# Attention and gated convolution on one core: q and k loaded nine tokens a row, five score matmuls a head, and a new written order

## The chip, the cores and the metric

The kernel runs on one core of one Trainium2 chip. The metric is the device time of one launch in microseconds. A core has five engines that run side by side, each through its own list of instructions in order: PE (matrix multiply; its weight loads are listed as PEld), ACT (activation functions and copies), DVE (elementwise work), POOL (GpSimd, which has no access to PSUM here) and SP (which only issues DMAs). They wait for one another through semaphores. Data moves between device memory and the on-chip memory (SBUF) by 16 DMA engines. PE writes into PSUM, which has eight banks of 128 partitions x 512 fp32.

## The reference

Attention with a block-causal mask over 8 batches, 8 heads, 576 tokens and a head size of 64, and behind it a gated unit: a causal convolution over 5 tokens makes a gate, a projection makes the values, and their product is projected out.

```python
# attention: q, k, v are (8, 8, 576, 64)
scores = (1 / sqrt(64)) * q @ k.T                 # per batch and head
mask   = (pos_q // 64) >= (pos_k // 64)
attn   = softmax(where(mask, scores, -1e9))
x      = (attn @ v) put as (B, S, 512)            # heads side by side
# gated unit
gate = sigmoid(sum over k of conv_w[k] * x shifted by 4 - k tokens)   # zeros ahead of each batch
out  = (gate * (x @ w_val)) @ w_out               # (8, 576, 512) fp32
```

## The kernel before, in words

The unit of attention is a pair of heads: pair p = 4 b + g holds heads 2 g and 2 g + 1 of batch b, so there are 32 pairs. The two heads of a pair lie on partitions 0 to 63 and 64 to 127, and PE works on both side by side. All work is cut into steps, and PLAN, a text of some 990 words, gives their order by hand. A word is `step/arguments/engine/banks`: `S/4.1/P/4+5` is step S for pair 4, pass 1, on PE, into banks 4 and 5. The loop at the end of the kernel emits the steps in that order; each engine gets its own steps in the order of the list, and a step waits for the data that it reads and for the banks or buffers that it overwrites. The engines are P (PE), A (ACT), V (DVE), G (POOL) and S (SP).

The steps of a pair:

- `lq`, `lk`, `lv` (SP): load q, k, v into rings of staging tiles (`qks`, `vs`, five each). Only tokens 0 to 511 go this way, four tokens a row of 1 KB. `cq`, `cv` cast to fp16.
- `T`: 16 transposes (64 x 64) of q and k; `Te` copies the result from PSUM to `qkT`. The first pair that is read in halves uses `T0`, `T0e`, `cq0`.
- The tail path: tokens 512 to 575 of q and k of a whole batch are loaded by `lt`, cast by `ct`, turned by `TT`, copied by `TTe` into `ktails`.
- `S`: scores in three passes of 512 columns, with keys on the partitions. Pass 0 is one matmul a head (512 columns), pass 1 two (384 and 128), pass 2 five (256, and four of 64 columns for the tail queries). `E` takes the exponential of one pass (128 x 1024 elements) on ACT. `SL` and `EL` do the tail keys with the tail queries for the whole batch.
- `mka`, `mkb` (POOL): memsets that put the mask's zeros into the result of E.
- `A`: 20 matmuls of 65 columns, attention times v with a column of ones; `N` divides by that column. `AT`, `NT` do it for the tail queries of a batch.
- `X` (and `XT`): transposes of the result; `Xe`, `XTe` copy it into `xt`, a ring of four batches with four columns of zeros ahead of each.

The gated unit runs over `xt` in ten runs n of 464 columns: `C` (80 matmuls in 32 x 32 tiles, four banks) is the convolution, `CS` the tanh on ACT (two a run), `V` (four a run) the projection by w_val, `Ve` the product on DVE into `gv`. `O` projects 128 tokens by w_out, `Oe` copies to an output tile, `Od` stores it. `OL` is the last output in two halves. C of a run needs Xe of all pairs of the batches that it covers, and V, Ve and O follow it.

At the start `CW` (on PE) turns conv_w, which `lcv` loads and `ccv` casts. `lwo`, `cwo` load w_out and cast it; step `W` puts its rows into the order of use by 16 matmuls, and `We` brings it back from PSUM with a factor 0.5.

PSUM is mostly given out in pairs of banks. A helper, `place`, lets several small results share a pair: T and SL take half of it, X and TT a quarter, A three quarters.

All matmuls and transposes are recorded at the lines of two helpers (`mm`, L137; `turn`, L141), and all copies at L246 (DVE and POOL) and L244 (ACT), so the profile tells them apart by the names of what they read and write: S reads `qkT`, A reads `v,pt`, C reads `xt,DG`, V `xt,w_val`, O `w_out,gv`; Te writes `qkT`, Xe `xt`, Oe `osb`.

Of the kernel before, what the change touches and what calls it, by code (L numbers as in the profile page):

```python
# [12 lines left out]
lk/1/S ppool//G pdve//V lcv//S ccv//G CW//P/1 lq/1/A cq/1/V T/1/P/4+5 lq/0/S lk/0/S lt/0.1/S  # L13
lt/0.0/S ct/0/G lk/4/S lq/3/S CWe//V lk/3/S cq/3/G cq0/0/V T0/0/P/0+1 lq/2/S lk/2/S lq/4/S cq0/1/V
T0/1/P/2+3 Te/1/A pact//A S/1.1/P/4+5 lv/1.0/S lv/0.0/S lv/0.1/S S/1.0/P/6+7 lt/1.0/S lq/5/S
lv/2.1/S T0e/0/V lk/5/S T0e/1/A S/0.0/P/2+3 lv/1.1/S lv/2.0/S lvt/0/S lv/3.1/S lt/1.1/S TT/0/P/0+1
lk/6/S TTe/0/V lv/3.0/S lq/6/S cq/4/G E/1.1/A E/0.0/A lwv/1/S lwv/0/S SL/0/P/0+1 EL/0/A S/0.2/P/2+3
E/1.0/A S/1.2/P/4+5 E/1.2/A S/0.1/P/0+1 T/3/P/6+7 cq/2/V T/2/P/4+5 mka/1/G cv/0/G Te/3/A S/3.1/P/6+7
E/0.1/A T/4/P/0+1 Te/2/V S/2.2/P/4+5 lwo/1/S lwo/0/S E/0.2/A mka/0/G mkb/0/G lk/7/S S/2.1/P/2+3
lq/7/S lt/2.0/S Te/4/V S/4.0/P/0+1 E/3.1/A E/2.2/A E/2.1/A S/2.0/P/6+7 E/2.0/A A/0/P/4+5 S/3.2/P/6+7  # L20
cq/5/V T/5/P/2+3 lt/2.1/S lk/8/S lv/4.1/S lq/10/S E/4.0/A N/0/V cv/2/V X/0/P/4+5 mkb/1/G cv/1/G
A/1/P/0+1 lq/8/S Xe/0/V E/3.2/A S/4.1/P/4+5 N/1/V S/3.0/P/6+7 mkb/3/G mkb/2/G mka/2/G Te/5/A
S/5.0/P/2+3 lk/10/S E/4.1/A ct/1/G cv/3/G lv/4.0/S A/2/P/0+1 N/2/V lq/9/S lk/9/S lv/6.0/S E/3.0/A
mka/3/G S/5.1/P/4+5 E/5.1/A TT/1/P/6+7 TTe/1/V lv/5.1/S cvt/0/G cq/6/G A/3/P/0+1 N/3/V cwv/1/G
cwo/0/G E/5.0/A ct/2/G lv/7.1/S S/4.2/P/6+7 SL/1/P/4+5 lv/6.1/S EL/1/A mka/4/G cq/7/G E/4.2/A
mkb/4/G cq/8/G lq/13/S lv/5.0/S lv/7.0/S lvt/1/S lk/12/S lq/12/S lk/11/S lq/11/S AT/0/P/2 X/1/P/4+5
X/3/P/0+1 Xe/3/A T/6/P/6+7 Te/6/A X/2/P/0+1 Xe/2/A NT/0/V XT/0/P/3 S/6.0/P/6+7 E/6.0/A Xe/1/V
C/0/P/0+1+4+5 CS/0.1/A CS/0.0/A XTe/0/V cwv/0/V V/0.3/P/7 cwo/1/V Ve/0.3/V V/0.0/P/6 Ve/0.0/V
S/6.1/P/4+5 E/6.1/A W//P/0+1+2+3 We/0/A We/1/V S/5.2/P/6+7 TT/2/P/4+5 TTe/2/V V/0.2/P/2 SL/2/P/0+1
S/6.2/P/4+5 E/5.2/A T/7/P/6+7 Ve/0.2/V Te/7/V EL/2/A E/6.2/A V/0.1/P/0 S/7.0/P/4+5 E/7.0/A mka/5/G  # L30
T/8/P/6+7 S/7.1/P/2+3 E/7.1/A Ve/0.1/V cv/4/G A/4/P/0+1 Te/8/V S/8.2/P/6+7 N/4/V E/8.2/A O/0.2/P/4
Oe/0.2/A mkb/5/G S/8.1/P/0+1 E/8.1/A X/4/P/2+3 mka/6/G cq/10/G Xe/4/V cq/9/G T/9/P/6+7 T/10/P/6+7
Te/9/V S/8.0/P/4+5 E/8.0/A O/0.0/P/2 Oe/0.0/V S/7.2/P/0+1 E/7.2/A S/9.2/P/4+5 E/9.2/A cv/6/G mkb/8/G
Te/10/V mkb/6/G A/6/P/2+3 cv/5/G A/5/P/0+1 N/6/V mka/7/G S/9.0/P/6+7 S/9.1/P/4+5 E/9.0/A mkb/7/G
cv/7/G A/7/P/2+3 lk/13/S E/9.1/A lt/3.0/S N/5/V X/5/P/2+3 S/10.1/P/6+7 E/10.1/A lq/14/S lt/3.1/S
cvt/1/G AT/1/P/0 S/10.0/P/4+5 E/10.0/A O/0.1/P/1 Oe/0.1/A lk/14/S N/7/V Xe/5/V NT/1/V XT/1/P/0
X/6/P/6+7 Xe/6/A XTe/1/V X/7/P/2+3 cq/12/G T/12/P/4+5 cq/11/G T/11/P/4+5 lv/9.1/S S/10.2/P/0+1
E/10.2/A cq/13/G mka/9/G Xe/7/V C/1/P/2+3+6+7 lv/8.1/S CS/1.0/A ct/3/G cq/14/G mka/8/G Te/11/V
Te/12/V lv/8.0/S lq/15/S cv/8/G mkb/9/G V/1.0/P/1 Ve/1.0/V V/1.1/P/0 Ve/1.1/V CS/1.1/A lk/15/S
lv/9.0/S lt/4.1/S S/11.1/P/2+3 lvt/2/S lv/11.1/S lt/4.0/S E/11.1/A lv/11.0/S lk/17/S T/13/P/4+5  # L40
TT/3/P/4+5 lq/17/S lv/10.0/S lv/10.1/S lq/18/S lk/18/S Te/13/V S/11.0/P/6+7 E/11.0/A V/1.3/P/1
Ve/1.3/V T/14/P/2+3 Te/14/V mkb/10/G cv/9/G lv/12.0/S mka/11/G S/11.2/P/6+7 V/1.2/P/0 TTe/3/A
E/11.2/A S/13.1/P/4+5 mkb/11/G lv/12.1/S Ve/1.2/V S/14.1/P/2+3 S/13.2/P/6+7 cq/15/G A/8/P/0+1
E/13.1/A O/0.4/P/4 ct/4/G E/13.2/A S/13.0/P/6+7 N/8/V E/14.1/A lq/16/S lk/16/S Oe/0.4/V A/9/P/0+1
S/12.0/P/2+3 X/8/P/4+5 E/13.0/A T/15/P/4+5 N/9/V S/12.1/P/6+7 S/12.2/P/0+1 E/12.0/A E/12.1/A
lv/13.1/S Te/15/V Xe/8/V X/9/P/2+3 E/12.2/A cv/11/G A/11/P/2+3 N/11/V O/0.5/P/7 lt/6.1/S Oe/0.5/A
Xe/9/V S/14.0/P/5+6 mka/10/G cvt/2/G lv/13.0/S cq/17/G TT/4/P/0+1 T/17/P/0+1 X/11/P/0+1 Te/17/V
mka/12/G E/14.0/A S/14.2/P/2+3 cv/10/G cq/18/G AT/2/P/7 E/14.2/A O/0.3/P/6 Oe/0.3/A TTe/4/V Xe/11/V
# [64 lines left out]
def kernel(  # L113
# [57 lines left out]
    def both16(banks):  # L171
        return pick(PS16, banks)
# [569 lines left out]
```

## Time and profile before

| | |
|---|---|
| device time, 3 runs | median 184.38 us (183.89 to 184.41) |
| span of the profiled execution | 180.0 us |
| the profiled execution's own time | not recorded apart from the runs; its span and what lies around it make up the runs' 184.4 us |
| DMA | 40.39 MB in 66494 packets |
| chain that ended last | PE 59%, DMA 14%, SP's queue 9%, ACT 6% |

The span runs from the first to the last instruction; a run's time also holds what lies around it, here about 4.4 us. The profile gives each engine's busy time, its idle time with what ended it, and the chain of work that ended last, which is followed back from the last instruction. The chain holds PE almost without a break from 74 us on; before that it passes through DMA landings, SP's issues, ACT and DVE.

### The profile page before, as it was taken

The page shows a single profiled execution, that of the slowest core. Times are in us where ns is not written, and L with a number is a line of the kernel's source. Part 1 is how long each engine was busy: PE and PEld are TensorE (multiplying, and loading weights), DVE is VectorE, ACT ScalarE, POOL GpSimd, SP SyncE. Part 2 cuts the span into 40 slices and gives each one's busy share as a digit, 9 for nine tenths or more (in the row PEclk, how much of TensorE's full clock was granted, in tenths as well). Part 3 has the DMA queues.
Part 4 walks back from the last instruction along what each step waited for, and adds up shares of the span by engine and source line. Part 5 has one row for each costly group of instructions (what it writes and reads, how often), then busy time and mean ns, then how long its engine had stood idle before and what let it go on. Part 6 is the DMA issues. An engine that isn't in the chain of part 4 may idle for free.

```text
span 180.0 us, 8228 instructions
## 1 busy us (share of the span) xinstructions
PE 159.7 (89%) x3513; PEld 98.5 (55%) x3513; DVE 122.6 (68%) x249; ACT 137.3 (76%) x162; POOL 82.6 (46%) x198
## 2 busy tenths in 40 slices
PE   0567987779989998899899999999999999999991
PEld 0343765345754665656555755566775557455450
DVE  6635665687869786669748896587984876935640
ACT  2499999889979997989798989988996753333432
POOL 6326372677674677547467437462930622000000
PEclk9999999999999999999999999999999999999999
DMA  5899899997978799969999997998796006063366
GB/s 171 255 302 228 195 326 358 267 271 171 292 223 233 175 281 243 236 200 269 296 214 273 329 275 193 293 284 224 229 319 167 0 4 230 6 232 127 117 235 232
DMA packets 66494, 40.39 MB, mean 224 GB/s; under 512 B 40213, under 2 KB 60949, under 8 KB 66458
## 3 DMA queue, kind: packets, MB, share of 16 engines
q1 hardware_dynamic: 65898, 39.35, 76.0%
q8 instruction: 27, 0.44, 1.1%
q10 hardware_dynamic: 560, 0.52, 0.9%
q14 instruction: 9, 0.07, 0.1%
HBM read 30.42 MB, written 9.44 MB: 221 GB/s over the span
## 4 chain that ended last, share of the span: by engine, by line
PE 59%; DMA 14%; SPq 9%; ACT 6%; issue 4%; DVE 3%; POOL 2%; POOLq 0%; DVEq 0%
PE PS L137 54%; PE PS L141 5%; DMA qks<-in_q_dram 5%; ACT pt L458 4%; SPq L258 4%; DMA qks<-in_k_dram 3%; DMA vs<-in_v_dram 3%; SPq L281 3%; SPq L274 2%; DMA conv_nat<-in_moe_conv_w_dram 2%; DMA vts<-in_v_dram 2%; ACT qkT L244 1%; DVE x L509 1%; DVE qkT L246 1%; POOL qk L246 1%
## 5 line engine op out<-in xcount | busy, mean ns | idle before, releaser
L458 ACT ACTIVATE pt<-PS 128x1024 f16<-128x1024 f32 x96 | 93.1, 1041 | 10.6 <-PE PS L137 9.0
L246 POOL CAST qk<-qks 128x1024 f16<-128x1024 f32 x28 | 29.0, 1041 | 18.8 <-DMA qks<-in_k_dram 9.1
L137 PE MATMUL PS<-xt,w_val 128*128 128x464 f16 x160 | 36.5, 360 | 0.5 <-DVE w_out L600 0.3
L137 PE MATMUL PS<-qkT 64*128 64x256 f16 (+3 forms) x256 | 34.0, 319 | 3.0 <-DVE qkT L246 1.2
L137 PE MATMUL PS<-w_out,gv 128*128 128x512 f16 (+1 forms) x148 | 35.6, 374 | 0.0
L635 DVE SCALAR_TENSOR_TENSOR gv<-th,PS 128x112 f16<-128x112 f32 (+4 forms) x64 | 26.1, 449 | 10.2 <-ACT th L617 5.1
L137 PEld LDWEIGHTS <-pt 128*128 128x128 f16 (+1 forms) x960 | 28.0, 103 | 8.0 <-issue 4.0
L137 PE MATMUL PS<-v,pt 128*128 128x65 f16 (+1 forms) x896 | 31.4, 196 | 0.8 <-POOL v L246 0.3
L246 DVE COPY qkT<-PS 128x1024 f16<-128x1024 f16 (+1 forms) x24 | 28.7, 1199 | 4.7 <-PE PS L141 3.0
L137 PEld LDWEIGHTS <-qkT 64*128 64x128 f16 x512 | 17.5, 98 | 16.6 <-issue 9.4
L617 ACT ACTIVATE th<-PS 128x928 f32<-128x928 f32 x20 | 17.8, 947 | 9.9 <-PE PS L137 9.5
L246 POOL CAST v<-vs 128x512 f16<-128x512 f32 x31 | 19.2, 622 | 12.0 <-DMA vs<-in_v_dram 8.7
L509 DVE TENSOR_TENSOR x<-PS,rc 128x512 f16<-128x512 f32 x32 | 22.1, 692 | 1.1
L137 PEld LDWEIGHTS <-w_val 128*128 128x128 f16 x160 | 13.9, 98 | 14.1 <-issue 2.6
L137 PEld LDWEIGHTS <-gv 128*128 128x128 f16 x148 | 13.0, 98 | 13.3 <-issue 1.5
L246 DVE COPY osb<-PS 128x512 f32<-128x512 f32 x18 | 12.4, 690 | 7.6 <-PE PS L137 5.2
L141 PE MATMUL PS<-ident,qk 64*128 64x64 f16 x512 | 13.8, 199 | 3.9 <-POOL qk L246 1.3
L246 DVE COPY xt<-PS 128x512 f16<-128x512 f16 (+1 forms) x34 | 13.1, 399 | 5.4 <-PE PS L141 3.2
L481 POOL MEMSET pt<- 64x256 f16 x32 | 9.8, 306 | 14.0 <-ACT pt L458 13.0
L244 ACT COPY osb<-PS 128x512 f32<-128x512 f32 x17 | 10.0, 586 | 7.0 <-PE PS L137 4.5
L141 PEld LDWEIGHTS <-qk 64*128 64x128 f16 x512 | 11.1, 100 | 7.2 <-POOL qk L246 2.8
L508 DVE RECIPROCAL rc<-PS 128x8 f32<-128x8 f32 x32 | 6.6, 205 | 12.2 <-PE PS L137 9.6
(62 smaller groups left out, 134.3 us busy)
## 6 DMA issues: line engine op xcount, KB each, us to landing
out_dram<-osb SPq DMA_DIRECT2D x35, 256.0 KB, 3.3
qks<-in_k_dram SPq DMA_DIRECT2D x32, 256.0 KB, 4.7
vs<-in_v_dram SPq DMA_DIRECT2D x64, 128.0 KB, 4.3
qks<-in_q_dram SPq DMA_DIRECT2D x31, 256.0 KB, 4.6
tls<-in_k_dram SPq DMA_DIRECT2D x16, 64.0 KB, 4.1
tls<-in_q_dram SPq DMA_DIRECT2D x16, 64.0 KB, 3.6
vts<-in_v_dram SPq DMA_DIRECT2D x8, 128.0 KB, 4.0
gv<-in_moe_w_val_dram SPq DMA_DIRECT2D x2, 512.0 KB, 6.9
```

Source lines behind the costliest of these rows:

```text
L137: made.append(nc.tensor.matmul(out=out, lhsT=lhsT, rhs=rhs, start=start, stop=stop, skip_group_check=True))
L141: made.append(nc.tensor.transpose(out=out, in_=in_, identity=identity))
L244: i = nc.scalar.copy(out=out, in_=in_)
L246: i = (nc.vector if eng == "V" else nc.gpsimd).tensor_copy(out=out, in_=in_)
L258: DMA[eng].dma_start(out=rot(qks, p)[0:128, i], in_=(q, k)[i][b, 2 * g:2 * g + 2, 0:512, 0:64].rearrange("h (p n) d -> p h (n d)", n=4))
L281: DMA[eng].dma_start(out=tls[b % 2][0:128, i, r], in_=(q, k)[i][b, 0:8, 512:576, 0:64].rearrange("(g r) (p n) d -> r p g (n d)", r=2, n=2)[r])
L458: made.append(nc.scalar.activation(out=rot(pts, p)[0:128, 0:2, 512 * t:512 * t + 512], in_=both(take("S", p, t)), func=AF.Exp, bias=0.0, s ...
L481: nc.gpsimd.memset(pt[64:128, 0:2, 0:1024].rearrange("p h (t s) -> p h t s", t=2)[:, :, :, 0:64], 0.0)
L508: made.append(nc.vector.reciprocal(out=rc[0:128], in_=r[:, :, :, 64:65]))
L509: made.append(nc.vector.tensor_tensor(out=rot(x16, p)[0:128].rearrange("p i h d -> p h i d"), in0=r[:, :, :, 0:64], in1=rc[0:128].to_broad ...
L617: made.append(nc.scalar.activation(out=rot(ths, n)[0:128, 2 * i:2 * i + 2], in_=both(take("C", n, i))[:, :, 0:RUN], func=AF.Tanh, bias=0.0 ...
L635: made.append(nc.vector.scalar_tensor_tensor(out=gv[0:128, x, a - 4 * i:e - 4 * i], in0=rot(ths, n)[0:128, x, a - o:e - o], scalar=1.0, in ...
```

## The change

- q and k are loaded with nine tokens in a row of 2304 bytes, all 576 tokens at once. `lt`, `ct`, `TT`, `TTe`, `ktails` are gone. For batch 0, `lq` and `lk` load a pair with q on partitions 0 to 63 and k on 64 to 127. From batch 1 on, `lQ` loads four heads (two pairs) of q or of k into one staging tile by two DMAs; the pairs' rows lie on the two halves of the partitions.
- `c` (or `ch` by halves) casts a staging tile, T does 18 transposes of it, Te copies 128 x 1152 elements. From batch 1 on one T is q or k of two pairs, so scores of a pair need two T.
- S has the passes 512; 448 and 64; 192 and 320 columns: five matmuls a head. Each mask step is one memset.
- `lwo` loads w_out in the order of use (four DMAs), `cwo` casts it with the factor 0.5. `W` and `We` are gone.
- `place` is gone: T, X, A and SL take a pair of banks each.
- The written order is new for all engines. It has filler matmuls at the start (`w0`: 6, 3, 2 and 1 of 512 columns on 128 rows), `ccv` on ACT, more casts on DVE (six `c`, ten `cv` and four `cvt`; before three `cq` and one `cv`), and nine stores (`Od`) on ACT's queue.

The order up to the first S passes of batch 1, and around C/2 and C/3, in the new list:

```diff
+lcv//S ccv//A lk/0/S pact//A pdve//V w0/6.128.0/P/7 CW//P/0 ppool//G lq/0/S ch/0.0/G ch/0.1/V lk/1/S
+lq/1/S c/1/G CWe//V w0/3.128.0/P/7 T/0/P/2+3 Th/0.0/A Th/0.1/V w0/2.128.0/P/7 S/0.1/P/2+3 E/0.1/A
+S/0.2/P/0+1 T/1/P/4+5 E/0.2/A w0/1.128.0/P/7 S/0.0/P/2+3 E/0.0/A Te/1/V lk/2/S lq/2/S lq/3/S lk/3/S
+lQ/2.0.0/S lQ/2.1.0/S lv/0.0/S lQ/2.1.1/S lQ/2.0.1/S lv/2.0/S lv/0.1/S lv/1.0/S lv/1.1/S lQ/3.1.1/S
+lQ/3.1.0/S c/2/G c/3/G T/2/P/0+1 S/1.2/P/4+5 E/1.2/A S/1.1/P/6+7 E/1.1/A Te/2/V S/1.0/P/2+3
...
+Xe/10/V Xe/11/V EL/3/A cv/12/V S/14.0/P/0+1 T/19/P/2+3 E/14.0/A Te/19/V C/2/P/4+5+6+7 cv/14/G
...
+Xe/14/V S/17.0/P/0+1 Te/20/V E/17.0/A C/3/P/2+3+6+7 C/4/P/0+1+4+5 CS/3.1/A CS/3.0/A V/2.3/P/6
```

The code, cut to its core:

```diff
+    NST, N16, NQT, NV, NV16, NPT, NX, NTH, NOSB = 6, 4, 3, 5, 7, 6, 4, 3, 6
...
-    qks = consts(5, [128, 2, 2, 256], fp32, "qks")
-    tls = consts(2, [128, 2, 2, 128], fp32, "tls")
+    st = consts(NST, [128, 2, 576], fp32, "st")
-    qk16 = consts(4, [128, 4, 4, 64], fp16, "qk16")
-    qkT = consts(4, [128, 2, 512], fp16, "qkT")
+    qk16 = consts(N16, [128, 9, 2, 64], fp16, "qk16")
+    qkT = consts(NQT, [128, 2, 2, 640], fp16, "qkT")
...
+    def load_early(i, p, eng):
+        DMA[eng].dma_start(
+            out=rot(st, p)[64 * i:64 * i + 64],
+            in_=(q, k)[i][0, 2 * p:2 * p + 2].rearrange("h (s n) d -> s h (n d)", n=9))
...
+    def lQ(u, i, h, eng="S", bank=None):
+        b, w = divmod(u, 2)
+        DMA[eng].dma_start(
+            out=rot(st, number(u, i))[0:128, h],
+            in_=(q, k)[i][b, 4 * w + h:4 * w + h + 3:2].rearrange("r (s n) d -> r s (n d)", n=9))
...
+    def lwo(x, eng="S", bank=None):
+        DMA[eng].dma_start(
+            out=w_out_st[0:128, x],
+            in_=moe_w_out.rearrange("(j x i) n -> x j i n", j=4, x=4)[x])
...
     def cwo(f, eng, bank=None):
-        copy(eng, w_out_16[0:128, 2 * f:2 * f + 2], w_out_st[0:128, 2 * f:2 * f + 2])
+        halved(eng, w_out_sb[0:128, 2 * f:2 * f + 2], w_out_st[0:128, 2 * f:2 * f + 2])
...
+    def T(k, eng, bank):
+        where["T", k] = bank
+        for n in range(9):
+            for r in range(2):
+                hs = slice(64 * r, 64 * r + 64)
+                turn(out=both16(bank)[:, r, 64 * n:64 * n + 64], in_=rot(qk16, k)[hs, n],
+                     identity=ident16[hs, hs])
...
+    def Te(k, eng, bank=None):
+        copy(eng, turned(k).rearrange("p r (s n) -> p r s n", n=9),
+             both16(take("T", k))[:, :, 0:576].rearrange("p r (n s) -> p r s n", n=9))
...
     def S(p, t, eng, bank):
-        if t == 0:
-            work = [(0, 0, 0, 512)]
-        elif t == 1:
-            work = [(0, 1, 128, 512), (384, 3, 384, 512)]
-        else:
-            work = [(0, 2, 256, 512)] + [(256 + 64 * j, j, None, None) for j in range(4)]
+        s, qt = both(bank), rot(qkT, p // 2)
+        work = (((0, 0, 0, 512),), ((0, 1, 128, 576), (448, 0, 512, 576)),
+                ((0, 3, 384, 576), (192, 2, 256, 576)))[t]
         for (o, j, a, e) in work:
             for h in range(2):
                 hp = slice(64 * h, 64 * h + 64)
...
+                mm(s[0:128, h, o:o + e - a], qt[hp, 1, p % 2, 128 * j:128 * j + 128],
+                   qt[hp, 0, p % 2, a:e])
...
-    def W(eng, bank):
...
-    def We(i, eng, bank=None):
...
```

More of the change, by code (lines that the diff above doesn't have):

```diff
@@ L312, in pdve @@
         nc.vector.tensor_copy(out=ident16[0:128], in_=ident[0:128])
-        for i in range(2):
-            nc.vector.memset(ktails[i][0:128, 0:4, 1:2, 64:128], 0.0)
+        for t in qkT:
+            nc.vector.memset(t[0:128, 1, 0:2, 576:640], 0.0)
         for i in range(4):
@@ L655, in Oe @@
     def Oe(u, t, eng, bank=None):
-        copy(eng, rot(osb, 9 * u + t)[0:128], one(take("O", u, t))[:, 0:512])
+        outs[u, t] = rot(osb, len(outs))
+        copy(eng, outs[u, t][0:128], one(take("O", u, t))[:, 0:512])
     @op
     def Od(u, t, eng, bank=None):
-        DMA[eng].dma_start(out=rows(u, t), in_=rot(osb, 9 * u + t)[0:128])
+        DMA[eng].dma_start(out=rows(u, t), in_=outs[u, t][0:128])
     @op
```

365 lines of the change are left out of this document (139 added, 226 removed).

## The prediction

> **What bounds the kernel now.** I read the page first, then the busy time by stretches, then PE in order of time.
>
> ```profile
> span 180.0 us, 8228 instructions
> ...
> PE 159.7 (89%) x3513; PEld 98.5 (55%) x3513; DVE 122.6 (68%) x249; ACT 137.3 (76%) x162; POOL 82.6 (46%) x198
> ```
>
> PE leads, but 89% is an average over stages. The stretches show them (columns: length, then PE, PEld, DVE, ACT and POOL busy, clock, DMA share, GB/s):
>
> ```profile
> core 0: us, PE busy (x) PEld busy (x) DVE busy (x) ACT busy (x) POOL busy (x), PEclk, DMA share, GB/s
> 0.00:6.00 6.00, 0.28 (x8) 0.27 (x10) 3.48 (x12) 1.28 (x1) 3.76 (x25) 1.00 0.65 203
> 6.00:30.00 24.00, 18.45 (x418) 12.65 (x419) 13.84 (x26) 22.53 (x28) 10.32 (x22) 1.00 0.94 275
> 30.00:52.00 22.00, 19.18 (x482) 11.88 (x451) 15.82 (x27) 18.80 (x22) 14.17 (x27) 1.00 0.89 248
> 52.00:75.06 23.06, 21.07 (x513) 13.70 (x510) 19.20 (x35) 21.17 (x25) 15.65 (x36) 1.00 0.89 231
> ...
> 100.00:130.00 30.00, 30.00 (x693) 18.99 (x693) 23.55 (x45) 27.16 (x32) 16.79 (x39) 1.00 0.93 256
> ...
> 176.34:180.00 3.66, 0.00 (x0) 0.00 (x0) 0.00 (x0) 0.58 (x1) 0.00 (x0) 1.00 0.53 195
> ```
>
> Until 75 us PE has holes, and ACT is the fullest engine: 22.53 + 18.80 + 21.17 = 62.5 of 69.1 us (90%). DVE does 48.9 us there (71%). From 100 us on PE has none: what is left for PE then is the time that is left. After PE's last instruction come 3.66 us of eviction and store. So time can be won where PE waits, before about 90 us, or by giving PE less to do.
>
> **Unit prices on PE.** A busy time holds the pipeline's modelled end, so I price a step by the distance from its start to the next start:
>
> ```profile
> 75.06 1.48 PE L137 MATMUL PS<-xt,DG 32*32 32x464 f16 x80
> ...
> 91.41 1.27 PE L137 MATMUL PS<-xt,DG 32*32 32x464 f16 x80
> 92.61 1.74 PE L137 MATMUL PS<-xt,w_val 128*128 128x464 f16 x8
> 94.28 0.28 PE L137 MATMUL PS<-qkT 64*128 64x256 f16 x2
> 94.40 0.28 PE L137 MATMUL PS<-kt,qkT 64*128 64x64 f16 x8
> 94.52 0.40 PE L141 MATMUL PS<-ident,qk 64*128 64x64 f16 x16
> 94.75 0.28 PE L141 MATMUL PS<-byhead,tl 64*128 64x64 f16 x8
> 94.87 0.40 PE L141 MATMUL PS<-ident,qk 64*128 64x64 f16 x16
> 95.20 1.04 PE L137 MATMUL PS<-w_out,gv 128*128 128x512 f16 x4
> 96.17 0.39 PE L137 MATMUL PS<-qkT 64*128 64x384 f16 x4
> ...
> 99.77 0.38 PE L137 MATMUL PS<-qkT 64*128 64x512 f16 x2
> 100.08 0.78 PE L137 MATMUL PS<-v,pt 128*128 128x65 f16 x20
> 100.70 0.95 PE L137 MATMUL PS<-xt,w_val 128*128 128x464 f16 x4
> 101.96 0.29 PE L141 MATMUL PS<-ident,x 64*128 64x64 f16 x8
> 102.07 0.65 PE L141 MATMUL PS<-ident,qk 64*128 64x64 f16 x32
> ```
>
> S (two heads side by side, 512 columns) takes 0.24 us when the next step has the same array shape (94.28 to 94.52) and 0.31 when it has not (99.77 to 100.08): a change of shape costs nearly 0.1. T 0.23, TT 0.12, X 0.11, A 0.62, V 0.79, O 0.87, C 1.1 without the change.
>
> **Five score matmuls a head.** The eight tail matmuls of 64 columns take 0.12 us (94.40 to 94.52), exactly as long as the two of 256 columns before them. PE pays for columns, and the new passes (512; 448 + 64; 192 + 320) have the same 512. I take 0; the two steps, read to 0.01 us, allow at most 0.02 us a pair either way, 0.6 us over 32 pairs. The Trainium skill (TensorEngine Tiling (Array Packing), Instruction Overhead) says that each matmul has about 60 cycles of overhead, so that one column costs as much as 60. At the page's 2.4 GHz that would be 25 ns for each of the three matmuls saved a head, the heads being side by side: an estimate of 2.4 us over 32 pairs. The rows above speak against it.
>
> **No tail path.** Gone are TT, TTe and `ct` (eight each), the 32 tail DMAs and their issues on SP. But T grows from 16 to 18 transposes, Te and the cast from 1024 to 1152 columns: the same elements, spread over the main path. What remains of the saving is fixed cost and queue work, and PE pays 18 x 0.23/16 = 0.26 instead of 0.23 + 0.12/4: nothing won. For DMA, two queue rows give the price of a packet:
>
> ```profile
> q1 hardware_dynamic: 65898, 39.35, 76.0%
> q10 hardware_dynamic: 560, 0.52, 0.9%
> ```
>
> 0.9% of 16 x 180 us is 26 us for 560 packets, 46 ns each at 930 B; 76% gives 33 ns at 597 B. A line through both: 10 ns a packet plus 0.039 ns a byte. The change turns 16384 packets of 1 KB and 4096 of 512 B into 8192 of 2304 B, 12288 fewer: an estimate of 123 us of engine time, 7.7 us on 16 engines, of 137. The bounds are 0 (all cost by byte) and 25 us (all by packet). Transfers are at 0.9 and more until 75 us, so this is room for ACT's inputs, not time by itself; I count no term for it.
>
> **W and We go; w_out comes in use order** with the 0.5 in its cast. One PE step, one ACT and one DVE eviction fall away, all before 75 us; they are in the counts below. SP gets four loads for two. One memset fewer a pair on POOL, which had slack (46%).
>
> **The start.** CW stands ahead of T/0 on PE as before and waits for conv_w:
>
> ```profile
> 1.25 3.49 DMA conv_nat<-in_moe_conv_w_dram
> 4.79 0.89 POOL conv L246
> ...
> 8.71 1.95 ACT L458 ACTIVATE pt<-PS 128x1024 f16<-128x1024 f32 x2
> 53.28 1.78 ACT L617 ACTIVATE th<-PS 128x928 f32<-128x928 f32 x2
> 59.10 6.52 ACT L458 ACTIVATE pt<-PS 128x1024 f16<-128x1024 f32 x7 [0.22 <-PE PS L137]
> ...
> 15.26 0.61 PE L141 MATMUL PS<-ident,qk 64*128 64x64 f16 x16 [0.32 <-ACT pt L458]
> 15.65 0.42 PE L137 MATMUL PS<-qkT 64*128 64x256 f16 x2
> ```
>
> (The first two from the chain, the rest from the timeline.) conv_w lands at 4.74, its cast moves to ACT (0.89 or a little less), then w0/3, T/0, Th, w0/2, S/0.1. T at 15.26 took 0.39 to the next start against 0.23 at 94.52, so early PE runs at about half pace, though the clock column says 1.00. At half pace the sum is 5.6 + 1.3 + 0.4 + 0.9 + 0.4 + 0.1 = 8.7, at full pace 7.7. I take 8.4 for the first E, 0.3 sooner than 8.71: ccv now holds ACT, and the twelve filler matmuls hold PE, but only where both waited. The Trainium skill (TensorE: Matmul & The Clock Gate, Part 1) says that about 3.4 us of sustained activity releases a half-rate gate; the fillers would give that early, which is the 7.7.
>
> **The order.** Here is the main term. I count the written lists up to a matched point: old C/2 (starts at 75.06) and new C/3. Evictions and casts are priced by these groups:
>
> ```profile
> L246 DVE COPY qkT<-PS 128x1024 f16<-128x1024 f16 x23 | 28.0, 1221 | 4.6 <-PE PS L141 2.8 <-ACT pt L474 1.5
> L509 DVE TENSOR_TENSOR x<-PS,rc 128x512 f16<-128x512 f32 x32 | 22.1, 692 | 1.1
> L246 DVE COPY xt<-PS 128x512 f16<-128x512 f16 x29 | 11.8, 418 | 2.6 <-PE PS L141 2.1 <-PE PS L137 0.4
> L244 ACT COPY osb<-PS 128x512 f32<-128x512 f32 x17 | 10.0, 586 | 7.0 <-PE PS L137 4.5 <-issue 2.4
> L244 ACT COPY qkT<-PS 128x1024 f16<-128x1024 f16 x8 | 8.2, 1027 | 4.8 <-PE PS L141 4.6
> L246 DVE COPY kt<-PS 128x512 f16<-128x512 f16 x6 | 4.3, 719 | 1.2 <-PE PS L141 1.1
> L246 DVE CAST qk<-qks 128x1024 f16<-128x1024 f32 x3 | 2.1, 694 | 4.1 <-DMA qks<-in_k_dram 3.5 <-DMA qks<-in_q_dram 0.6
> ```
>
> ACT ahead of that point: 53 E for 51 (+2 x 0.93), 6 CS for 4 (+2 x 0.89), 4 Te of 1152 for 5 of 1024 (-0.5), 1 Oe for 4 (-1.8), and of small copies -1.7, an estimate at 0.59 for 128x512 and 1.03 for 128x1024 as in the two ACT rows (two Xe, TTe and We fewer, ccv and XTe more). Sum -0.3: the same work. None of the nine Od that move to ACT's queue stands ahead of that point.
>
> PE after that point: 16 A for 18 (-1.2), 4 AT for 5 (-0.6, by A's price), 7 C for 8 (-1.1), 31 V for 32 (-0.8), 30 O for 29 (+0.9), 43 S for 45 (-0.5), 11 T for 13 T and 3 TT (-0.5), 16 X for 20 (-0.4), two XT fewer (-0.2), 68 changes of shape for 76 (-0.7). Sum -5.1. The old rest took 176.34 - 75.06 = 101.3 us, the new should take 96.2. In all both orders have 133 changes of shape.
>
> DVE ahead of that point: 16 N for 14 (+1.8, with 0.2 for each reciprocal), 16 Te of 1152 for 13 of 1024 (+6.1), no TTe for 4 (-2.9), 15 Xe for 9 (+2.5), two Oe more (+1.4), four v casts more (+1.6), and +0.3 for the rest (NT, Ve and XTe one more each, We and the early casts less). Sum +10.8, so 59.7 us instead of 48.9.
>
> If ACT alone set the pace, C/3 would start at 75.06 - 0.3 - 0.3 = 74.4. Then DVE must be busy 59.7 of 68.4 us from 6.0 on, 87%. It reached 83% in 52 to 75 and 78% in 100 to 130. The lost packing pulls the same way: T, X, SL and A now hold a whole pair of banks until DVE or ACT has copied it out, and S behind them waits for that. So I let both cost a little and take C/3 at 76.0 (85%). PE ends at 76.0 + 96.2 = 172.2, the span at 175.9 with the same 3.66 behind it. The runs shown (median 184.38) lie 4.4 over the profiled span; the profiled execution's own time is not shown, and I give it that median. Forecast **180.3**.
>
> **Rivals.** (1) DVE becomes the bound, slower. N, Xe and Te free the banks that PE needs next, and casts of q, k and v now stand between them in DVE's queue. At 78.5%, its share in 100 to 130, 59.7 us need 76.0, C/3 starts at 82.0, the time is 186.3. It decides from C/3 at 80.1 on, a share below 81%. For it: no stretch before 75 us shows more than 83%. Against: much of its idle time there was waiting for PE and ACT.
> (2) Inputs by twos, slower. From batch 1 on a score pass needs four transfers of 288 KB for two pairs, not two of 256 KB for one: 0.64 MB more, at the 248 GB/s of 30 to 52 us 2.6 us. If that shows at two units, 184.38 - 4.1 + 5.2 = 185.5. Against: SP has 32 issues less, the ring holds six tiles.
> (3) Better: DVE manages 90%, C/3 at 72.3, time 176.6.
> (4) The matmul overhead is real, and the score merging gives its 2.4 us, some 1.4 behind C/3: 178.9.
> (5) The front-loading buys nothing, since PE's holes move behind C/3: no change, 184.
>
> **Numbers.** Forecast case (C/3 at 73 to 79, 177.3 to 183.3) 0.52, (3) 0.10, (4) 0.03, (5) 0.05, (1) 0.22, (2) 0.08. About 0.3% is what a measurement here can tell from no change. Faster 0.65, same 0.05, slower 0.30. The range 175.5 to 187.0 takes in (3) and the rivals' prices and leaves out their far ends; the likeliest case alone has 177.3 to 183.3.
>
> **What would show it.** S passes still 0.24 us to the next start, first E at 7.7 to 8.7, C/3 at 73 to 79, PE without holes behind it, some 96 us to its last matmul, and DVE at 83 to 88% from 6 us to C/3. Wrong: C/3 after 80 with PE waiting for DVE (rival 1) or for casts that wait for DMA (rival 2), or new holes in PE behind 100 us.

## The result, and the profile after

| | us |
|---|---|
| kernel before, on the same chip | 184.13 (183.63 to 184.41, 4 runs) |
| changed kernel | **468.83** (468.31 to 470.08, 4 runs) |
| ratio | 2.548, 95% interval 2.536 to 2.560 |
| forecast | 180.3 (175.5 to 187.0) |

The changed kernel takes two and a half times as long. Its page (span, busy time, DMA's slices and packets, the first queue, the chain that ended last):

```profile
span 467.4 us, 7721 instructions
...
PE 210.2 (45%) x3316; PEld 116.4 (25%) x3316; DVE 127.3 (27%) x253; ACT 140.6 (30%) x163; POOL 70.4 (15%) x142
...
DMA  7222221324112321112311222412232542350206
...
q1 hardware_dynamic: 51274, 37.24, 26.3%
...
DMA 42%; SPq 36%; PE 15%; issue 2%; POOL 2%; DVE 2%; ACT 1%; POOLq 0%; ACTq 0%; DVEq 0%
```

DVE and ACT have about as much to do as before (127 us for 123, 141 for 137), and PE's 210 us hold fewer instructions than before (3316 for 3513). The engines wait. 78% of the chain are transfers and SP's queue, yet the DMA row stands mostly at one to three tenths. The last column of the queue row makes it sharper. 26.3% of 16 engines for 467.4 us is 1967 us of engine time; before it was 76.0% of 16 x 180.0, which is 2189. So the transfers cost *less* engine time than before and still hold everything up. The waits show what for (engine, line, what ended the wait: us in all, times, longest):

```profile
POOL qk L228 <- DMA st<-in_q_dram: 166.5, 13, 39.1
PEld L139 <- POOL qk L228: 156.2, 18, 18.7
ACT pt L408 <- PE PS L135: 153.2, 40, 24.4
```

The cast waits for q, the transposes for the cast, the exponential for the scores. A stretch in which only `lQ` transfers are under way gives the reason; first the stretch (PE, PEld, DVE, ACT, POOL busy, clock, DMA share, GB/s), then the DMA view of the same stretch:

```profile
238.00:259.00 21.00, 3.58 (x76) 2.91 (x76) 1.99 (x5) 3.06 (x4) 1.15 (x1) 0.59 0.13 50
```

```profile
DMA packets 460, 1.04 MB, mean 50 GB/s; under 512 B 8, under 2 KB 8, under 8 KB 460
...
q1 hardware_dynamic: 460, 1.04, 13.1%
```

13.1% of 16 engines are 2.1 engines. These 460 packets took 0.131 x 16 x 21.0 / 460 = 96 ns each, about the 100 ns of the prediction's line for 2304 B. The packets are as cheap as forecast, but only two engines carry them. One `lQ` then lasts 128 x 96 / 2 = 6.1 us and the 56 of them 344 us of the 467. SP cannot run ahead either; its issues take microseconds. First the issues of q in the kernel before and in the changed one (count, min/median/max ns), then some of the changed kernel in order of time (start, length):

```profile
L258 SPq DMA_DIRECT2D qks<-in_q_dram x31: 367/505/1795, 1.7 to 123.7; - x31
L265 SPq DMA_DIRECT2D st<-in_q_dram x28: 526/3330/9291, 6.5 to 398.9; - x28
```

```profile
16.46 2.91 SPq L265 DMA_DIRECT2D st<-in_k_dram  x1
19.42 4.02 SPq L265 DMA_DIRECT2D st<-in_q_dram  x1
23.48 12.99 SPq L272 DMA_DIRECT2D vs<-in_v_dram  x4
```

The v loads (L272) are the same as before; they stand in SP's queue behind `lQ`.

Why two? The source of `lQ` is written `"r (s n) d -> r s (n d)"`, and r, the outermost dimension, has size 2. The Trainium skill (DMA: Bandwidth & Descriptors, Why a DMA increments its semaphore by 16 and not by 1) says that a transfer runs on the largest number of engines up to 16 that divides the slowest dimension of both access patterns. By that rule `lQ` has two engines and `lwo`, whose source starts with j = 4, has four; the old loads had 128 rows outermost and 16 engines. The rows above agree for two; the experiments below vary the number.

### The profile page after: what moved, and what is told of

Read it like the earlier page. It is cut to its first block, busy times and chain, and to the rows that moved or that the text cites. A ratio compares the mean times of both kernels' runs of the same rounds, so it can differ in the third digit from the quotient of the medians.

```text
span 467.4 us, 7721 instructions
## 1 busy us (share of the span) xinstructions
PE 210.2 (45%) x3316; PEld 116.4 (25%) x3316; DVE 127.3 (27%) x253; ACT 140.6 (30%) x163; POOL 70.4 (15%) x142
## 3 DMA queue, kind: packets, MB, share of 16 engines
q1 hardware_dynamic: 51274, 37.24, 26.3%
## 4 chain that ended last, share of the span: by engine, by line
DMA 42%; SPq 36%; PE 15%; issue 2%; POOL 2%; DVE 2%; ACT 1%; POOLq 0%; ACTq 0%; DVEq 0%
DMA st<-in_q_dram 18%; DMA st<-in_k_dram 17%; SPq L272 16%; PE PS L135 14%; SPq L265 13%; DMA vs<-in_v_dram 7%; SPq L278 5%; SPq L593 1%; POOL qk L228 1%; SPq L283 1%; PE PS L139 1%; POOL v L228 0%; DVE x L460 0%; DVE qkT L228 0%; SPq L247 0%
## 5 line engine op out<-in xcount | busy, mean ns | idle before, releaser
L408 ACT ACTIVATE pt<-PS 128x1024 f16<-128x1024 f32 x96 | 94.4, 1024 | 163.8 <-PE PS L135 153.2
L228 POOL CAST qk<-st 128x1152 f16<-128x1152 f32 (+1 forms) x26 | 29.3, 1128 | 266.1 <-DMA st<-in_q_dram 166.5
L228 DVE COPY qkT<-PS 128x1152 f16<-128x1152 f16 (+1 forms) x25 | 33.2, 1331 | 72.1 <-PE PS L139 67.2
L135 PE MATMUL PS<-qkT 64*128 64x64 f16 (+4 forms) x384 | 46.3, 346 | 13.7 <-ACT pt L423 5.6
L135 PE MATMUL PS<-v,pt 128*128 128x65 f16 (+1 forms) x896 | 40.5, 217 | 20.1 <-POOL v L228 15.8
L135 PE MATMUL PS<-xt,w_val 128*128 128x464 f16 x160 | 45.0, 423 | 7.8 <-DVE xd L487 4.0
L135 PE MATMUL PS<-w_out,gv 128*128 128x512 f16 (+1 forms) x148 | 44.0, 443 | 4.5 <-DVE rc L459 4.5
L135 PEld LDWEIGHTS <-pt 128*128 128x128 f16 (+1 forms) x960 | 36.9, 118 | 31.2 <-issue 22.0
L567 DVE SCALAR_TENSOR_TENSOR gv<-th,PS 128x112 f16<-128x112 f32 (+6 forms) x64 | 25.7, 448 | 19.9 <-PE PS L135 15.8
L226 ACT COPY qkT<-PS 128x1152 f16<-128x1152 f16 (+1 forms) x8 | 8.5, 1058 | 61.8 <-PE PS L139 61.8
L228 POOL CAST v<-vs 128x512 f16<-128x512 f32 x22 | 13.8, 631 | 75.0 <-DMA vs<-in_v_dram 34.1
L428 POOL MEMSET pt<- 64x256 f16 x64 | 18.7, 320 | 19.4 <-ACT pt L408 17.8
```

What stands on the lines that cost most here:

```text
L135: made.append(nc.tensor.matmul(out=out, lhsT=lhsT, rhs=rhs, start=start, stop=stop, skip_group_check=True))
L226: i = nc.scalar.copy(out=out, in_=in_)
L228: i = (nc.vector if eng == "V" else nc.gpsimd).tensor_copy(out=out, in_=in_)
L408: made.append(nc.scalar.activation(out=rot(pts, p)[0:128, 0:2, 512 * t:512 * t + 512], in_=both(take("S", p, t)), func=AF.Exp, bias=0.0, s ...
L428: nc.gpsimd.memset(rot(pts, p)[64:128, 0:2, a:a + 2 * step].rearrange("p h (t s) -> p h t s", t=2)[:, :, :, 0:64], 0.0)
L567: made.append(nc.vector.scalar_tensor_tensor(out=gv[0:128, x, a - 4 * i:e - 4 * i], in0=rot(ths, n)[0:128, x, a - o:e - o], scalar=1.0, in ...
```

## The experiments

The theories: **A**, the outermost dimension of the source sets the number of engines; **P**, transfers to half of the partitions are dearer; **O**, the new order, the score merging or the fillers cost the time. The expectations use more letters, and each says what they mean. Times are medians of four executions, unless a number is given; the kernel before took 182 to 185 us beside them, on several chips.

**The cause put alone into the kernel before.** Its q and k loads are cut in two by heads, 128 rows each; only the way in which the source is written differs between the four kernels (b2, b4 and b8 so take the tokens in another sequence). b16 was executed twice, the others once.

```diff
-            in_=(q, k)[i][b, 2 * g:2 * g + 2, 0:512, 0:64].rearrange("h (p n) d -> p h (n d)", n=4))
+        for h in range(2):                                   # b16
+            ... in_=(q, k)[i][b, 2 * g + h, 0:512, 0:64].rearrange("(p n) d -> p (n d)", n=4))
+            # b2, b4, b8: "(s r n) d -> r s (n d)", r = 2, 4, 8
```

> Control: the kernel before, with each load of q and k cut into two by heads (128 partitions, 128 rows of 1 KB each); the output stays the reference's. 64 more issues on SP, everything else the same. All theories: 183 to 192.

> b16 with the rows of a head taken in another sequence, so that the outermost dimension of the source has 2 rows (2 x 64 rows of 1 KB); the tokens of q and k then lie in another sequence, so scores are masked and summed for other tokens than the reference's. Same number of transfers, issues, bytes, rows and destinations as b16. Theory A: 64 tiles x 256 rows x 46 ns on 2 engines are 377 us, and the rest of the traffic adds its sixteenth: 390 to 450 us. Theories B and C: as b16.

> The kernel before with its q and k loads cut by heads (as in the control, 202.6) and the source read with outermost dimension 4. Theory A: 128 transfers of 128 rows at 46 ns on 4 engines are 128 x 128 x 46 / 4 = 188 us where outermost 2 had 377; outermost 2 took 461 = 377 + 84, so 188 + 84 = 272, less what the other engines take beside it: 230 to 275. Rival (the order in which the rows are read costs, whatever the number of engines): near 461. Rival (only two is bad): near 203.

> As the last, with outermost dimension 8. Theory A: 94 + 84 = 178 us, which is under the control's 202.6 that other work sets, so 203 to 212. Rival (the order of the rows): near 461.

| outermost | 2 | 4 | 8 | 128 (b16) |
|---|---|---|---|---|
| us | 461.25 | 289.75 | 217.35 | 202.64 |

Spans and first queues of b2, b4, b8 and b16:

```profile
span 459.5 us, 8320 instructions
...
q1 hardware_dynamic: 65142, 39.34, 28.1%
```

```profile
span 288.0 us, 8320 instructions
...
q1 hardware_dynamic: 65394, 39.34, 45.4%
```

```profile
span 215.6 us, 8320 instructions
...
q1 hardware_dynamic: 65898, 39.35, 61.6%
```

```profile
span 200.4 us, 8320 instructions
...
q1 hardware_dynamic: 66906, 39.35, 69.9%
```

The engine time is 2066, 2092, 2125 and 2241 us: nearly the same work, spread over fewer engines. From two to four rows the time falls by 172 us, from four to eight by 72, where halving 377 us of transfers on two engines gives 188 and 94. All four lie above my bounds: b2 and b16 by 11 us, b4 by 15 and b8 by 5. So the sum "transfers by their engines, plus 84 us" is too simple, but the order of rows as such (b4 would stay at 461) is out.

The packet counts give the number of engines without any time. The queue carries 126 of these transfers. From b2 to b4 it has 252 packets more, from b4 to b8 504, from b8 to b16 1008: 2, 4 and 8 for each transfer, as if each engine that takes part added one packet. By the same count each of the 56 `lQ` has 14 engines more in e1 below than in the changed kernel (52058 - 51274 = 784 = 56 x 14), and `lwo` had four (g1's queue has 240 packets more than e5's, 16 x 16 - 4 x 4). In the quiet stretch above, the 8 packets under 512 B fit the ends of four transfers on two engines each.

Theory A is shown in a kernel that has nothing else of the change. b16 also has a price of its own, some 18 us over the kernel before, where I expected 8 at most: it has 63 more issues on SP's queue and 52 us more engine time (3 us on 16 engines); no run separates the two.

**The changed kernel with 16 engines for q and k.** In e1 each transfer fills one half of the partitions; in e5 it loads two neighbouring heads as one run of 128 rows. e5 has the instructions of a kernel with its heads paired anew, but not that kernel's result: its scores meet another head's v, and so do those of g1 to g7, which build on it.

```diff
-            out=rot(st, number(u, i))[0:128, h],
-            in_=(q, k)[i][b, 4 * w + h:4 * w + h + 3:2].rearrange("r (s n) d -> r s (n d)", n=9))
+            # e1: out=rot(st, number(u, i))[64 * h:64 * h + 64]
+            # in_=(q, k)[i][b, 4 * w + 2 * h:4 * w + 2 * h + 2].rearrange("h (s n) d -> s h (n d)", n=9)
+            # e5: out as before the edit
+            # in_=(q, k)[i][b, 4 * w + 2 * h:4 * w + 2 * h + 2].rearrange("r (s n) d -> (r s) (n d)", n=9)
```

> The changed kernel with one edit: each lQ loads the two heads of one pair into one half of the partitions (source rows outermost 64) instead of one head of each of two pairs into all of them (source rows outermost 2). Same number of transfers, bytes, rows of 2304 B, order and waits; the output stays the reference's. Theory A (a transfer is dealt out to as many DMA engines as its outermost source dimension allows, so lQ runs on 2 of 16): the stall goes, 173 to 188 us, DMA share 0.8 and more in the first 75 us, SP issues of 0.5 to 0.7 us. Theory B (rows of 2304 B are slow, or slow to issue): stays near 468. Theory C (the new order, inputs by twos): stays near 468, since neither the order nor the wait for four transfers changes. If A holds, the prediction's own sum (180.3) is tested here for the first time: C/3 at 73 to 79 us.

> The changed kernel with one edit: each lQ loads two neighbouring heads, whose 128 rows of 2304 B are one run in device memory, so the source is one dimension of 128 rows and the destination all 128 partitions. Same number of transfers, bytes, rows, order and waits. It gives q and k of heads h and h+1 the places of h and h+2, so scores meet another head's v: a stand-in for a re-paired kernel, with the same instructions. Theory A+P (2 engines in the changed kernel; in e1 all 16, but writing to 64 partitions at a time is slow): rows of 2304 B take 90 to 110 ns instead of e1's 175, and 256 B rows 18 ns instead of 29; 174 to 186 us. Theory S (rows of 2304 B on 16 engines are slow): 160 ns and more, 215 to 230 us. Theory C (what is left over in e1 is the new order): packets fast, but still 215 to 230 us.

e1 took 225.99 us (224.62 to 227.85; ratio 1.237, 1.229 to 1.245), e5 197.23 (196.74 to 197.88; 1.070, 1.064 to 1.077). Writing this one load another way takes away 243 or 272 of the 285 us, but both stay above what I expected (188 and 186 at most). e1 and e5 move the same packets; their first queues and the issues of q (count, min/median/max ns) differ. The first two rows are e1's, the last two e5's:

```profile
q1 hardware_dynamic: 52058, 37.25, 79.5%
```

```profile
L265 SPq DMA_DIRECT2D st<-in_q_dram x28: 595/605/3158, 6.5 to 167.4; - x28
```

```profile
q1 hardware_dynamic: 52058, 37.25, 69.8%
```

```profile
L265 SPq DMA_DIRECT2D st<-in_q_dram x28: 328/432/1281, 6.5 to 135.1; - x28
```

With spans of 224.5 and 195.9 us that is 2856 us of engine time in e1 and 2188 in e5, 42 us on 16 engines, and 173 ns more for an issue, 10 us over 56. So theory P has two prices, and together they more than cover the 28.8 us between the kernels. That it is the half of the partitions is not shown by this pair alone, because e1 also reads the rows of two heads in turn and e5 in one run. The kernel before reads in turn as well, to all 128 partitions: its engine time is 2189 us where b16, head by head, has 2241, so the order of the rows costs nothing there, but its issues take 505 ns where b16's take 432. By that, some 70 of the 173 ns would be the form of the source. The same cut in the kernel before:

```diff
+        for r in range(2):                                   # f1
+            ... out=rot(qks, p)[64 * r:64 * r + 64, i]
+            ... in_=(q, k)[i][b, 2 * g:2 * g + 2, 256 * r:256 * r + 256, 0:64].rearrange("h (p n) d -> p h (n d)", n=4))
```

> The kernel before, with each load of q and k cut into two of 64 partitions each (128 rows of 1 KB each); the output stays the reference's. Theory P: rows of 1 KB take 70 to 90 ns instead of 46 to 53, and the time rises to 195 to 225 us, although size of rows and order are the old ones; 64 more issues of some 0.5 us on SP are part of it, which b16 bounds. Theory S: only the issues cost, 184 to 195.

f1 took 224.81 us (two executions; ratio 1.220, 1.212 to 1.229), 22 more than b16 with as many transfers. Here the engine time is 2304 us against 2241, which is 4 us on 16. The rest fits the issues: 126 of 607 ns in the median where b16 has 431, which is 22 us, with SP's queue at 41% of the chain instead of 26%. So the larger part would be packets in e1 and issues in f1; no run separates the two.

**w_out by 16 transfers of 32 rows**, from e1 (e2) and from e5 (g1):

```diff
-            out=w_out_st[0:128, x],
-            in_=moe_w_out.rearrange("(j x i) n -> x j i n", j=4, x=4)[x])
+        for j in range(4):
+            ... out=w_out_st[32 * j:32 * j + 32, x], in_=moe_w_out[128 * j + 32 * x:128 * j + 32 * x + 32])
```

> e1 with w_out's rows loaded by 16 transfers of 32 rows (64 KB) in place of 4 of 128 rows whose outermost source dimension is 4; the output stays the reference's. Theory A: the four ran on 4 engines, 128 rows of 2 KB at 84 ns on 4 engines are 2.7 us each instead of 0.7; in e1 they stand behind batch 2's loads, so 0 to 3 us faster than e1 if a load behind them is late there, and 12 more issues of some 0.5 us on SP take part of it back: e1 -2 to +2. Theories B and C: no change against e1.

> The kernel of e5 (q and k loaded as one run of 128 rows, two neighbouring heads a transfer, so that the scores of one head meet the values of another) with w_out by 16 transfers of 32 rows in place of 4 transfers whose outermost dimension is 4. Theory A (a transfer runs on as many engines as its outermost dimension allows): w_out was on 4 engines and was waited for (6 us on VectorE and 6 us on GpSimd in e5); the same edit took 6.3 us from e1, so 197.2 - 6 = 191 (188 to 193). Rival O (what e5 keeps over the kernel before is the new order itself, its masks, its copies or its score passes): w_out's waits are only moved, 196 to 198.

e2: 219.64 us (ratio 1.191, 1.181 to 1.202), 6.4 less than e1 by the medians and 8 by the ratios, where I expected 2 at most. g1: 192.43 (191.38 to 194.1; 1.058, 1.050 to 1.067), 4.8 less than e5 and near the 191 that theory A gave. But e5 and g1 ran on two chips, on which the kernel before took 184.28 and 182.35; by the ratios the gain is some 2 us, and their intervals overlap. The waits are clearer. e5's waits for w_out are gone in g1:

```profile
DVE w_out L235 <- DMA osb<-in_moe_w_out_dram: 6.2, 1, 6.2
POOL w_out L235 <- DMA osb<-in_moe_w_out_dram: 5.8, 1, 5.8
```

**Score merging and fillers**, both on e1:

```diff
-                ((0, 3, 384, 576), (192, 2, 256, 576)))[t]
+                ((0, 3, 384, 512), (128, 3, 512, 576), (192, 2, 256, 512), (448, 2, 512, 576)))[t]   # e3, pass 1 alike
```

> e1 with the score passes cut into eight matmuls a head as before the change (512; 384, 64, 64; 128, 64, 256, 64), same columns; the output stays the reference's. Cost by columns (the prediction): e1 within 0.6 us. Cost of 60 cycles a matmul: 2.4 us more PE work, e1 +1 to +2.4.

> e1 without the twelve filler matmuls at the start; the output stays the reference's. Prediction: they only move PE between half and full pace early; first E between 0.7 us sooner and 0.5 later, total e1 -0.5 to +1.5. A rival: with PE at half pace up to about 20 us the first passes feed ACT late, e1 +2 or more.

e3 took 228.25 us (227.5 to 228.58), e4, which drops the four `w0` words from PLAN, 225.54 (224.33 to 227.57). The intervals of both ratios overlap e1's; against 285 us both are nothing.

**What keeps g1 ten us above the kernel before?** g2 to g5 try the start: batch 0's `lq` on ScalarE's queue (g2), no `w0` (g3), `lq` on that queue ahead of all else (g4), both (g5).

```diff
-... lcv//S ccv//A ... w0/6.128.0/P/7 ... lq/0/S ... lq/1/S ... lq/2/S lq/3/S
+... lcv//S ccv//A ... lq/0/A ... lq/1/A ... lq/2/A lq/3/A            # g2, in the old places
+... lcv//S lq/0/A lq/1/A lq/2/A lq/3/A ccv//A ...                    # g4; g3 drops w0; g5 does both
```

> The kernel of g1 with batch 0's four loads of q issued by ScalarE's queue instead of SyncE's, so that transfers to the lower 64 partitions (q) and to the upper 64 (k) are under way together. Theory P (a transfer to 64 partitions alone is slow by packet, 161 ns against 96): batch 0's eight transfers have 8 x 128 packets that cost 65 ns too much, on 16 engines 1024 x 65 / 16 = 4.2 us; with both halves written together most of it comes back, so g1 less 3 (0 to 5), about 188. Rival O: SyncE's issues (0.4 to 0.6 us each) and not the packets set the start, then four issues fewer ahead give up to 2 us; and if neither, the same time as g1 within 1 us.

> The kernel of g1 without the filler matmuls (w0) in the first microseconds. In g1 the granted clock is 0.64 from 6 to 30 us, in the kernel before 1.00, and in e4, which had no fillers, 1.00 up to 40 us. Theory C (the clock costs g1 part of its 10 us): PE is busy 17.5 of these 24 us; at full clock some of that work ends sooner, 2 us less than g1, 190.4 (188 to 191.5). Theory D (the start waits for transfers, DMA share 1.04 to 1.20 from 5 to 25 us): no change, 191.5 to 193.

> The kernel of g1 with the four loads of batch 0's q issued first of all on ScalarE's queue (in g2 the last two stood behind its first activations and were issued at 13.7 us). Theory P (transfers to 64 partitions alone are slow): q and k run together as in g2, where 5 to 15 us moved 277 and 312 GB/s against 229 and 250 in g1; the 2.36 MB of the first eight transfers then end about 1.7 us sooner: 190.7 (189 to 192). Rival (four issues of 0.65 us ahead of ScalarE's first work delay it by as much): 193 to 195.

> Both changes on g1. If both theories C and P hold, 188 to 190; if neither, 192 to 194. Near or below 184 only if the rest of g1's excess over the kernel before is in the start, which the distance after the fourth conv step (106.7 us in g1, where 99.9 was forecast) speaks against.

g2 took 199.09 us (197.4 to 201.79), 7 more where I expected 3 less: its third and fourth `lq` stood behind the first activations in ScalarE's list and were issued only at 13.7 us. g3 took 191.83, g4 192.55, g5 193.99, with ratios of 1.050, 1.059 and 1.062 and intervals that overlap g1's. The clock column did rise; 6 to 30 us of g1 and of g5:

```profile
6.00:30.00 24.00, 17.50 (x307) 10.22 (x307) 15.76 (x21) 17.97 (x20) 11.72 (x20) 0.64 1.10 269
```

```profile
6.00:30.00 24.00, 16.84 (x306) 10.41 (x307) 16.12 (x21) 18.06 (x20) 12.12 (x21) 1.00 1.04 273
```

PE's pace did not rise with it. One step A (20 matmuls of 65 columns) near 23 us, in the kernel before, in g1 and in g5:

```profile
22.99 0.77 PE L137 MATMUL PS<-v,pt 128*128 128x65 f16 x20
23.74 1.28 PE L135 MATMUL PS<-v,pt 128*128 128x65 f16 x20
23.65 1.28 PE L135 MATMUL PS<-v,pt 128*128 128x65 f16 x20
```

At 18.20 us it took 1.28 in the kernel before too. So a column of 1.00 does not mean full pace this early, and g3 and g5 do not test what a faster PE would give at the start. They do not clear the start either. In these 24 us ACT does 17.97 us of work in g1 and 22.53 in the kernel before (the prediction's row). Up to the matched point ACT idles for 16.9 us in g1 and 6.6 before, so 4.6 of the 10.3 us more are lost by 30 us. What is shown is only that none of these edits brings C/3 forward by more than 0.6 us: it starts at 86.03 in g1, 93.16 in g2, 86.91 in g3, 85.46 in g4 and 85.62 in g5.

The last three take loads of v away, to see whether supply is:

```diff
     def lv(p, h, eng="S", bank=None):
+        if p >= 5 and p % 2: return      # g6 (on g1) and b6 (on the kernel before); g7: if p >= 5
```

> The kernel of g1 without 28 of the 64 loads of v (those of the odd pairs from 5 on; those pairs use what lies in the buffer). Theory S (the new order asks for inputs sooner than the transfers bring them): up to the fourth conv step the new list uses 21 tiles of q and k of 590 KB and v for 16 pairs, the old list up to its third one 19 pairs of 524 KB, 5 tails of 262 KB and v for 14 pairs: 1.6 MB more, 6.6 us at the 248 GB/s that the kernel before moved up to there. The loads left out are 28 x 512 packets at 20 ns, 18 us of 16 engines; so g6 loses most of g1's excess: 183 (180 to 186). Rival E (the order of VectorE's, GpSimd's and ScalarE's work sets it): 190 to 193.

> As g6, with 54 of the 64 loads of v left out (all from pair 5 on). Theory S: supply no longer binds and the order shows what it gives by itself, near the forecast: 180 (176 to 183). Rival E: 188 to 192.

> The kernel before with the same 28 loads of v left out as in g6. Theory S: its transfers are at 0.88 and not above 0.99 either, but PE is busy without a hole from 75 us on, so it wins less than g6: 180 (177 to 182). Rival F (any kernel here wins as much by fewer bytes, so that supply is not what sets the two orders apart): as many us less as g6, about 175.

g6 took 191.62 us (190.86 to 193.8), g7 189.29 (189.15 to 194.64; ratio 1.041, 1.031 to 1.051), b6 had a ratio of 1.000 (0.993 to 1.006, ten executions). Theory S, supply, falls for most of the ten us: with 54 of 64 loads of v gone, some 3 us come back, and the intervals of g1 and g7 just touch. C/3 does not come sooner in g7 (86.96); what came back lies behind it. C/3 and PE's last group in g1:

```profile
86.03 2.06 PE L135 MATMUL PS<-xt,DG 32*32 32x464 f16 x116
181.72 7.08 PE L135 MATMUL PS<-w_out,gv 128*128 128x512 f16 x36
```

From C/3 to PE's end g1 needs 188.80 - 86.03 = 102.8 us, g3, g5 and g6 100.6 to 100.8, g7 96.8 (below), where 96.2 was forecast. So with all loads in place part of the excess lies behind C/3. g7's profile says where the rest is. Up to the matched point, first the kernel before (6 us to C/2), then g7 (6 us to C/3):

```profile
6.00:75.06 69.06, 58.71 (x1373) 38.24 (x1374) 48.86 (x87) 62.50 (x74) 40.14 (x84) 1.00 0.90 252
```

```profile
6.00:86.60 80.60, 66.82 (x1499) 42.42 (x1500) 58.50 (x105) 63.02 (x70) 46.93 (x74) 0.94 0.88 250
```

ACT's work is the same (62.5 and 63.0 us). PE is busy for 8.1 us more and idle for 13.8 us instead of 10.4. What PE waited for in g7 up to there, and C/3 and PE's last group:

```profile
PE PS L135 <- issue: 5.4, 3, 2.3
PE PS L135 <- DVE qkT L228: 2.0, 3, 1.5
PE PS L139 <- DVE convT L531: 1.8, 1, 1.8
```

```profile
86.96 2.04 PE L135 MATMUL PS<-xt,DG 32*32 32x464 f16 x116
...
176.70 7.08 PE L135 MATMUL PS<-w_out,gv 128*128 128x512 f16 x36
```

C/3 starts at 86.96, 11.9 us behind the old C/2. Of that 8.1 us are PE's longer busy time and 3.4 more idleness (the stretch ends at 86.60), in which 5.4 us of "issue" appear that the kernel before does not have there (its longest PE wait after 6 us is 1.9 in all). "Issue" is time for which the profile shows no cause; no run here acts on it, so it stays open. That PE kept its share (85% before, 83% in g7) is a reading of the rows; no run here moved PE's work alone. Behind C/3, g7 needs 183.78 - 86.96 = 96.8 us to PE's end, 4.5 less than the old 101.3. So only some 4.5 of the 8.1 us were moved ahead; the other 3.6 are added. PE's half pace may be part of them, since it lasts longer than before (A at 23.81 us still takes 1.28 in g7); no run shows how much.

## Why the prediction was wrong, point by point

**The step that failed** is the last sentence of "No tail path": the new loads were priced by packets and bytes, and "I count no term for it". The price of a packet was right: 100 ns by my line, 96 measured. The number of engines was not in the sum at all. I divided by 16 without looking at the outermost dimension of the new source, though the diff shows it. The bounds "0 to 25 us" allowed only gains. The missing term is 128 x 96 ns x 56 x (1/2 - 1/16) = 301 us of transfer time, and undoing it (e5) took 272 us away.

**The last term of the sum,** 4.4 us for what lies around the span, was too large as well: in every later execution on record the time is 1.7 to 2.0 us above that execution's own span. The profiled execution of the kernel before, whose own time was not recorded, was by that one of some 182 us, not of the median 184.38.

**Rival (2), inputs by twos,** named the right kind of wait (a cast that waits for DMA), with 5.2 us for it. It asked how many bytes a score pass needs, not how fast a transfer moves.

**DMA's saving.** Apart from the engines, the saving of 7.7 us did not come. In g1:

```profile
q1 hardware_dynamic: 52298, 37.25, 71.7%
```

Over a span of 192.3 us this is 2206 us of engine time against 2189 before, with 13600 packets fewer, of which 1024 net have only moved to ACT's queue with the stores. A packet took 42 ns in the mean, for 712 B, where my line gives 38. Why is not shown.

**The order.** "If ACT alone set the pace, C/3 would start at 74.4." In the changed kernel C/3 came at 261.56, so the order can only be judged in the g kernels. The counts of work held there: ACT 63.0 us for 62.2 expected and DVE 58.5 for 59.7 in g7. The 96.2 us behind C/3 held only in g7, without most of v (96.8); g1 took 102.8. The inference did not hold. I put 5 us of PE's work ahead of the matched point and never asked whether PE had room there. It had 10.4 us of holes, and it kept them. C/3 came at 86.96 in g7 and 86.03 in g1 instead of 76.0, late by more than rival (1) had (82.0). That DVE is the reason is not shown: its share is 73%, not 85. Rivals (3) and (4) needed C/3 at 76 or sooner. Rival (5), holes that move behind C/3, came in part: g1 has 4.3 us of "issue" in PE behind C/3, but the holes ahead of it stayed too.

**The start.** The first E came at 9.66 us in the changed kernel, outside 7.7 to 8.7:

```profile
9.66 1.94 ACT L408 ACTIVATE pt<-PS 128x1024 f16<-128x1024 f32 x2 [0.90 <-PE PS L135]
```

conv_w was not what it waited for, as I had assumed; it was cast by 2.93. Batch 0's casts waited until 6.55 and 6.61 us for q:

```profile
6.61 0.66 POOL L228 CAST qk<-st 128x576 f16<-128x576 f32 x1 [3.07 <-DMA st<-in_q_dram]
```

**Five score matmuls.** At full pace in g7 a pass of 448 and 64 columns takes 0.23 us to the next start, as forecast:

```profile
131.46 0.39 PE L135 MATMUL PS<-qkT 64*128 64x448 f16 x4
131.69 0.28 PE L139 MATMUL PS<-ident,x 64*128 64x64 f16 x8
131.80 0.38 PE L135 MATMUL PS<-qkT 64*128 64x512 f16 x2
```

Eight matmuls a head instead of five (e3 against e1) cost 2.3 us, about the 2.4 that I estimated from the overhead of the Trainium skill (TensorEngine Tiling (Array Packing), Instruction Overhead). But both kernels wait for inputs and their ranges touch, so neither my 0 nor the page's price is settled. In either case it is no part of the result.

**The clock.** I cited the Trainium skill (TensorE: Matmul & The Clock Gate, Part 1) for fillers that release a half-rate gate early. The runs agree for one step in one of two profiles, and show no gain in time: T/0 took 0.67 us at 7.45 in the changed kernel and 0.44 at 7.22 in g1, both with fillers, and 0.67 at 7.18 in g3 without; the first E came at 9.66, 9.39 and 9.35. From 10 to 24 us g1 and g3 take the same times for the same steps (T 0.66 at 10.12 and 10.08), although the clock column says 0.50 in the one and 1.00 in the other. The column is 1.00 in the first 5 us with and without fillers too, where the first six fillers take 0.45 us each and four later matmuls of 512 columns take 0.87 together. Why PE went back to half pace is open.

## What to carry to other kernels

Before pricing a load by its bytes, read the outermost dimension of both its access patterns and put the 128 rows there; one run of 128 rows (e5) did better here than transfers to halves (e1). A low DMA share together with a chain of DMA waits and with issues of several microseconds on the queue meant too few engines here, not too many bytes; in a stretch in which such a load alone is under way, the share times 16 was their number, and the packet counts of two kernels gave it too. When work is moved ahead, add it to each engine's work ahead of the matched point: PE was 85% busy there, did not fill its holes, and C/3 came later. And take an engine's pace from the length of a step that you know, not from the clock column alone.

## What the runs showed of the hardware that was not expected

- A transfer whose source has 2 rows outermost ran on 2.1 engines at 50 GB/s; the time of a whole kernel goes from 203 to 217, 290 and 461 us with 128, 8, 4 and 2 rows outermost, at nearly the same engine time, and its packet count falls by 8, 4 and 2 for each transfer.
- Transfers to 64 partitions went with 605 ns instead of 432 for an issue of q and with 31% more engine time (2856 against 2188 us) for the same packets in e1 and e5; in f1 the engine time rose by 3% over b16. e1 and e5 also differ in the order in which rows are read.
- The kernel before with 63 more issues on SP's queue, 431 ns each in the median, took some 18 us longer (b16).
- 54 of 64 loads of v could be left out of g1 for 3 us, with DMA shares of 0.9 and more up to 125 us: a high DMA share did not mean that supply was the bound.
- The clock column can say 1.00 while PE is at half pace: A took 1.28 us at 23.65 us in g5 (column 1.00 from 6 to 30 us) and 0.77 at 22.99 us in the kernel before.
